# A hyena filter prepared in thirteen buffers of its own and copied out whole: gated recurrence and long convolution on one core

## The chip, the core and the metric

The kernel runs on one core of one Trainium2 chip. The metric is device time in microseconds (us) from the start of a launch to its end; less is better. The engines of a core that matter here are PE (TensorE, the matmuls; PEld is its loading of weights), DVE (VectorE), ACT (ScalarE), POOL (GpSimd) and SP (SyncE, which here only issues DMA transfers). PSUM is the memory that PE writes, in 8 banks of 512 float32 per partition; SBUF is the working memory of 128 partitions; HBM (also called DRAM below) lies outside the core.

## The reference

Two models in a chain. The first is a gated recurrence over 6272 time steps, the second multiplies two projections of its result with a third one that was convolved with a filter of full length.

```python
# x, f_logit: (4, 6272, 256); lower_bound: (256)
sig = 1.0 / (1.0 + np.exp(-f_logit))
f = lower_bound + (1.0 - lower_bound) * sig
for t in range(S):
    h = f[:, t] * h + (1.0 - f[:, t]) * x[:, t]
    y[:, t] = h
# second model, x = y: w_proj (256, 768), filter_fft (6272, 256), w_out (256, 256)
proj = x @ w_proj
x1, x2, x3 = proj[..., :D], proj[..., D:2*D], proj[..., 2*D:]
X2 = np.fft.rfft(x2, n=S, axis=1)
H = np.fft.rfft(filter_fft, n=S, axis=0)
x2_conv = np.fft.irfft(X2 * H, n=S, axis=1)
out = (x1 * x2_conv * x3) @ w_out
```

All inputs and the output are float32.

## The kernel before

*The transform.* S = 6272 = 128 x 49 (`M` and `Q`), so a transform of the whole length is done as two rounds of matmuls, over 128 and over 49, with tables of sines. What has no partner in this split, frequency 0 of each row, is carried by a small extra path ("mini", "zm", "slot").

*Preparation (`prepare`), once.* The filter comes from HBM in 13 groups of four values of r (0 to 48; `ff`, L619), each 128 x 1024 float32, 0.524 MB. They go into 10 buffers in turn (`raws`, L438 to L442, and L618: `raws[g % len(raws)]`): seven in the space of `X2`, two in `Hu`, one in `HA`; groups 10, 11 and 12 wait until a buffer is free. A cast writes a group to one of two halves of `afs` (`fr`, L625), a matmul per r rotates it (`rot`, L630, with the table `rot` that `turns` copies from the identity), and two copies per group (`f2`, L634), one per half p of the columns, take it from PSUM to one of two tiles `f2`. The first transform of the filter (`FF1`, L655, 16 steps u of 8 columns pairs, two ops each) needs all 13 groups of its half of the columns; a copy (`afs`, L660), the second transform (`FF2`, L673) and a copy (`hw`, L677) follow; every two steps the spectrum is stored to a table in DRAM (`hst`, L682) of 192 rows: 128, and once more 64 in turned order. Later each batch loads a step's spectrum back with `turned` (L276), 128 rows from row 0 and 128 from row 49. The zero frequency is done by `last` (L691).

The tables are computed on the chip: integers (`iotas`, POOL, L487 on), arguments folded into one period (`args0`, `args1` and `fold`, DVE, L515 on), a sine on ACT, then the tables `D1r` and `FTr` for the filter ("tabs": three DVE and two POOL operations) and `D1`, `FT`, `VA`, `VB`, `ID` for the batches ("rest", POOL). Their scratch space lies in `A` and `PP`. The weights are scaled by 1 - lower_bound and cast to half precision by seven ACT operations ("W", L477 to L487). PE runs 24 fillers (`warm`, L600, four matmuls on the identity, nothing reads them); before, 10 of them stand ahead of the first FF1 and 14 at the very end.

*Recurrence (`hgrn`, L319), per batch.* 13 chunks of 512 steps: loads of f_logit and x (L332) into slots, a sigmoid (ACT, L335), u = sigmoid * x (POOL, L337), transposes for two halves kh of the channels (`su`, PE, L349), f (`f`, ACT L362 or DVE L364), the scan (DVE, L370) into `HA`. The first 3072 steps of `HA` are copied once more behind its end ("wrap", L379, on ACT, POOL or by a DMA of SP), as the circular convolution reads past it. Batch 0 has four slots for its input: three of its own and one in `XS`, the space where x1 and x3 are laid later; batches 1 to 3 have three.

*Convolution, per batch.* `phase_p` projects x2 (P, L714, 13 groups of four r, each needs all scans) and copies it to `X2` ("x2"). 16 units u follow: F1 (L727) with the copy A, F2 (L790), the product with the spectrum, which is loaded by SP into `Hu` (three places and one more in `Hl`, "H", L768), then the back transform I2 (L832) and the copy `Th`. The product is either made by DVE straight from PSUM (L813, in the order table MUL) or by a copy on ACT or DVE and a multiply on POOL (`pm`, L822). `gate` makes x1 and x3 (x13, PE, L398): x1 is copied to `XS`, and x3 is either multiplied straight from PSUM by DVE (L419) or copied, with the product z on POOL (L428). `phase_o` does the last transform (I1, L895), the product with z (y, DVE, L901), the output projection (proj, L913), a copy ("o") and the store (L925). The scans of the next batch run under the units and the gate of this one.

*What sets the order.* No scheduler works at build time. Every piece of work is an operation `op(kind, cost, ...)` with a number; the table `ORDER` (a string of base 64 digits at the top of the file) lists for all 2429 operations their number, engine and PSUM bank, and `Plan.emit` issues them in that order. `cost` names the engines on which an operation may run; which one it gets stands in the table. Each engine and SP's queue of transfers work strictly in the order of the table. The core of it:

```python
for i, e, b in self.order():
    o = self.ops[i]
    assert e in o["cost"] and i not in seen and o["preds"] <= seen
    ...
    o["fn"](*args)
```

Of the kernel before, what the change touches and what calls it, by code (L numbers as in the profile page):

```python
# [2 lines left out]

# [6 lines left out]
F32 = mybir.dt.float32  # L10
F32R = mybir.dt.float32r
F16 = mybir.dt.float16
# [48 lines left out]
class Plan:  # L61
# [63 lines left out]
    "AAYAvQAeQAOYAzYAiQAnQAoQA0gA1AAfQA5gA6YA+gAqQBDgAjQBIgBNgABIACIAPIARIAQAAUIAWIA2QA/YA3AA4AATIA7SBEYBXgA8CA9CBAUB"  # L125
    "JYBCEBFWBOYBHGBBEBGGBKQBLABMIBPSBYYBQCAVYAXYBSgBTAAwUBRKAdUBZUBaEBUWBWGBVOBhgBiYBcgBdYBjQBbEBeSBgCBkABrgBsIBtUAS"
    "ABmgBnIBoWBfKBuEBwgBxIBySBvEBpOBqOBzCB5UB6MAYYAZYADgEGgB0CD6gD8AD7gB3SB+WB4KD5gAEYB/OB1YBlICAUCBECJSEIAEHgB8WB9G"
    "B7YCKKCCYD9YEegCDQCEIEJYESgETgCQUEgACHSCREAFgCOWCIKCLYCPOCSYD+QEUACMSCNCCTUCUEEfgAGgECWEqgErgCZSCaCCGgD/IEAIEDOE"
    "EOEVYEKQCXUEhYAHACeSELAAIAEOWE3gE2gCYMCbYCfCEMIEPGEQOAJACgUCcSChECiYCdCEWQCjUCkEEaWFCgAaYCpSEXIEYIEbGEcOCqCEsACW"
    "gEiUEjMEtYCmgCnQCoAFDgCrYCwSEkMCuWCxCCvGCyYEmQEnIFMgFNgCzSE4AEoIE5YC0CCsUCtEEuWGJgEZYEvOFEAFFYCFgEySFWgEzKFXgC3Q"  # L130
    "C4AEwOExYC5UC6EE0KALAE6QC7YE7AFOADAUC+WDBMFPYC/GDCYE8IE9YE+SFggE/CFhgFAKC8UC9EAKAFGWFHGDDQDEIDFgFIODHUDIEAMAE1YF"
    "BYFJSFKCFqgDJQFrgEdYEpgDKIDLYDOUFYAFZYDPEDQWDRGB2YFQQFTUF0gF1gFLKFiADSYDMSDNCDTWDUGFaSFRIC1gFUMFSIFbCDXQDgWDYAFV"
    "MFcKFjYDZUFdQANADaMDbYDhOFsAF/gFtYFkSFeAFfIDcUFlCFmKDdEF+gDVgFnWMsgMtgF2AClgDeQDfIDnUFoGDoEFpOFuSFvCDjQFwKDkAFxU"
    "M5gFyEFzMDpWDqGM4gF3YF4QF5AF6IF7SDiYDrYGAAJdWGIgJfGDuUEBYDwWF8CGBYDvEEFYDxGDyYERYF9KJeQJiRJgoGCUGFWElYJhYJkBMggM"
    "hgGGGGHOGDEGEMC2gENADsSDGgDzQD0ID3WDtCD1gD2gD4OGZUGaECVgGbSMuAGcCGfQGgAGhUGiMMiAMjYM6AGLWGdSGeKGMGGNQGOAGVUGWMM7"
    "YGPSGQKJjWJluJmYJnXGjQGkAMvYGXUDmgGYEGTQGKgGUAJpPGRSGSKDWgJoUJsVJtQJxRJqEJrYJzJJvADlgGrSGlWJyUGmOJuFJwYJ2VGsCGnQ"
# [58 lines left out]
def kernel(  # L195
# [801 lines left out]
```

## Time and profile before

| | us |
|---|---|
| runs of the kernel before | 459.30, 458.43, 457.25 (median 458.43) |
| span of the profiled execution | 455.6 |
| first rotation of the filter starts | 6.28 |
| first FF1 starts | 22.82 |
| last input of batch 0 has landed | 64.75 |
| last scan of batch 0 starts | 70.8 |
| first P of batches 0, 1, 2, 3 | 71.5, 167.1, 266.0, 366.0 |
| last output projection ends | 450.4 |
| last store lands | 454.2 |

The page shows one profiled execution; its span runs from the first to the last instruction, and the runs without a profile are some 2 to 4 us longer than that. The groups of the page's fifth part give the count, the busy time and the mean of one operation by line and form; the ones with most time on each engine are these:

```profile
L337 POOL TENSOR_TENSOR XT<-XT,FL 128x1024 f32<-128x1024 f32 (+1 forms) x49 | 109.9, 2247 | 55.7 <-ACT FL L335 38.5
L370 DVE TENSOR_TENSOR_SCAN HA<-fTs,HA,PS 128x512 f16<-128x512 f32 (+1 forms) x96 | 112.7, 1202 | 2.0 <-ACT fTs L362 1.1
L398 PE MATMUL PS<-HA,W 128*128 128x490 f16 (+1 forms) x416 | 100.2, 367 | 0.3 <-ACT Th L284 0.2
...
L284 ACT CAST HA<-PS 128x1024 f16<-128x1024 f32 (+1 forms) x101 | 81.2, 831 | 3.3 <-POOL PP L822 0.8
```

So the 96 scans take DVE 112.7 us, 1.202 us each, and before them DVE stood idle for 2.0 us in all, mostly until ACT had written `fTs`. Nearly all the copies from PSUM go through one helper, `copy`, whose lines are L284 and L286 on ACT and the like on DVE; there the tile, not the line, tells what is copied.

### The profile page before, as it was taken

The page shows a single profiled execution, that of the slowest core. Times are in us where ns is not written, and L with a number is a line of the kernel's source. Part 1 is how long each engine was busy: PE and PEld are TensorE (multiplying, and loading weights), DVE is VectorE, ACT ScalarE, POOL GpSimd, SP SyncE. Part 2 cuts the span into 40 slices and gives each one's busy share as a digit, 9 for nine tenths or more (in the row PEclk, how much of TensorE's full clock was granted, in tenths as well). Part 3 has the DMA queues.
Part 4 walks back from the last instruction along what each step waited for, and adds up shares of the span by engine and source line. Part 5 has one row for each costly group of instructions (what it writes and reads, how often), then busy time and mean ns, then how long its engine had stood idle before and what let it go on. Part 6 is the DMA issues. An engine that isn't in the chain of part 4 may idle for free.

```text
span 455.6 us, 14635 instructions
## 1 busy us (share of the span) xinstructions
PE 439.6 (96%) x6009; PEld 348.4 (76%) x6009; DVE 407.4 (89%) x476; ACT 402.3 (88%) x577; POOL 308.8 (68%) x279
## 2 busy tenths in 40 slices
PE   7899999999999999999999999999999999999998
PEld 5687778677767888777668888777778896776797
DVE  8899997799999996999999977999999976989873
ACT  5899999899999987899989998999989858987563
POOL 8888973878899542788995626899994405696400
PEclk9599999999999999999999999999999999999999
DMA  8999999767898985479776896778759721765186
GB/s 326 387 371 345 378 375 361 279 187 233 299 300 282 340 300 237 169 232 374 253 264 219 285 315 272 237 250 303 261 177 317 301 95 46 248 187 185 47 321 246
DMA packets 44434, 120.74 MB, mean 265 GB/s; under 512 B 4304, under 2 KB 7632, under 8 KB 44368
## 3 DMA queue, kind: packets, MB, share of 16 engines
q1 hardware_dynamic: 44368, 119.82, 74.5%
q8 instruction: 47, 0.77, 0.7%
q14 instruction: 19, 0.16, 0.1%
HBM read 86.12 MB, written 31.98 MB: 259 GB/s over the span
## 4 chain that ended last, share of the span: by engine, by line
PE 72%; DVE 11%; ACT 9%; issue 4%; DMA 3%; POOL 1%; SPq 0%; ACTq 0%; DVEq 0%; POOLq 0%
PE PS L398 17%; PE PS L714 9%; PE PS L832 9%; PE PS L913 8%; PE PS L790 7%; DVE HA L370 7%; PE PS L727 6%; PE PS L349 6%; PE PS L895 4%; ACT fTs L362 2%; DMA X<-in_moe_filter_fft_dram 2%; PE PS L600 2%; ACT HA L284 2%; DVE ys L901 1%; ACT X L284 1%
## 5 line engine op out<-in xcount | busy, mean ns | idle before, releaser
L337 POOL TENSOR_TENSOR XT<-XT,FL 128x1024 f32<-128x1024 f32 (+1 forms) x49 | 109.9, 2247 | 55.7 <-ACT FL L335 38.5
L370 DVE TENSOR_TENSOR_SCAN HA<-fTs,HA,PS 128x512 f16<-128x512 f32 (+1 forms) x96 | 112.7, 1202 | 2.0 <-ACT fTs L362 1.1
L398 PE MATMUL PS<-HA,W 128*128 128x490 f16 (+1 forms) x416 | 100.2, 367 | 0.3 <-ACT Th L284 0.2
L822 POOL TENSOR_TENSOR PP<-HA,Hu 98x1008 f16<-98x1008 f16 x42 | 88.0, 2106 | 5.6 <-ACT HA L284 2.6
L284 ACT CAST HA<-PS 128x1024 f16<-128x1024 f32 (+1 forms) x101 | 81.2, 831 | 3.3 <-POOL PP L822 0.8
L901 DVE TENSOR_TENSOR ys<-PS,zt 128x1024 fp32r<-128x1024 f32 (+1 forms) x52 | 58.3, 1151 | 14.0 <-PE PS L895 10.3
L813 DVE TENSOR_TENSOR PP<-PS,Hu 98x1008 f16<-98x1008 f32 x54 | 63.6, 1199 | 1.5 <-PE PS L790 0.7
L362 ACT ACTIVATE fTs<-PS,nomc 128x512 f32<-128x512 f32 (+1 forms) x90 | 59.5, 680 | 4.5 <-PE PS L349 4.2
L398 PEld LDWEIGHTS <-W 128*128 128x128 f16 x416 | 35.3, 97 | 30.2 <-issue 2.9
L428 POOL TENSOR_TENSOR zt<-XS 128x490 f16<-128x490 f32 (+1 forms) x26 | 31.8, 1223 | 39.0 <-DVE ys L901 27.4
L913 PE MATMUL PS<-Wo,ys 128*128 128x256 f32 x392 | 57.5, 293 | 0.4 <-DVE ys L901 0.3
L286 ACT ACTIVATE XS<-PS 128x490 f32<-128x490 f32 (+1 forms) x88 | 51.0, 590 | 6.8 <-DVE zt L419 2.6
L832 PEld LDWEIGHTS <-PP 98*128 98x128 f16 x1024 | 49.2, 98 | 10.1 <-POOL PP L795 1.3
L284 ACT CAST Th<-PS 128x784 f16<-128x784 f32 x63 | 52.0, 828 | 3.4 <-PE PS L832 2.7
L913 PEld LDWEIGHTS PS<-Wo,ys 128*128 128x128 f32 x392 | 49.6, 188 | 4.5 <-DVE ys L901 1.2
L832 PE MATMUL PS<-VA,PP 98*128 98x98 f16 x512 | 52.1, 207 | 0.2 <-POOL PP L795 0.2
L832 PE MATMUL PS<-VB,PP 98*128 98x98 f16 x512 | 51.8, 207 | 0.0
L419 DVE TENSOR_TENSOR zt<-PS,XS 128x490 f16<-128x490 f32 (+1 forms) x78 | 49.2, 648 | 2.7 <-ACT XS L286 0.8
L335 ACT ACTIVATE FL<-FL 128x1024 f32<-128x1024 f32 (+1 forms) x49 | 49.8, 1022 | 0.6 <-DMA FL<-in_f_logit_dram 0.6
L714 PE MATMUL PS<-W,HA 128*128 128x256 f16 x392 | 44.6, 273 | 1.1 <-ACT X L284 1.1
L714 PEld LDWEIGHTS <-HA 128*128 128x128 f16 x392 | 42.9, 142 | 2.0 <-issue 1.3
L349 PE MATMUL PS<-iden,FL 64*128 64x64 f32 x736 | 41.7, 229 | 2.6 <-ACT PP L286 0.6
(119 smaller groups left out, 778.7 us busy)
## 6 DMA issues: line engine op xcount, KB each, us to landing
FL<-in_f_logit_dram SPq DMA_DIRECT2D x45, 512.0 KB, 5.3
XT<-in_x_dram SPq DMA_DIRECT2D x45, 512.0 KB, 6.2
Hu<-H SPq DMA_DIRECT2D x39, 512.0 KB, 4.6
out_dram<-osb SPq DMA_DIRECT2D x24, 512.0 KB, 4.6
out_dram<-PP SPq DMA_DIRECT2D x16, 512.0 KB, 4.8
Hl<-H SPq DMA_DIRECT2D x13, 512.0 KB, 4.7
X<-in_moe_filter_fft_dram SPq DMA_DIRECT2D x9, 512.0 KB, 7.0
out_dram<-HA SPq DMA_DIRECT2D x8, 512.0 KB, 5.7
```

What stands on the lines that cost most here:

```text
L284: nc.scalar.copy(dst, src)
L337: op("u", {"POOL": 0.1 + 0.553 * nb}, lambda e, xt=xt, ft=ft: nc.gpsimd.tensor_tensor(xt, xt, ft, op=AOP.mult), r=[("ft", k)], w=[("xt", k)])
L349: nc.tensor.transpose(bank(pb)[:, at[p] + j:at[p] + hn:nb], src[ps, j, cols], iden[ps, ps])
L362: nc.scalar.activation(fT, sT, AF.Identity, scale=by, bias=1.0)
L370: nc.vector.tensor_tensor_scan(h, fT, bank(pb)[:, 512 - hn:512 + hn], init, op0=AOP.mult, op1=AOP.add),
L398: nc.tensor.matmul(PS[:, p, 0:n], W13[:, kh, js], HA[:, HB[kh] + t0:HB[kh] + t0 + n], start=(kh == 0), stop=(kh == 1))
L714: nc.tensor.matmul(pp[:, r - r0, :], column(HB[kh], q_of(r)), W2[:, kh, :], start=(kh == 0), stop=(kh == 1))
L813: nc.vector.tensor_tensor(pr, px.unsqueeze(1).broadcast_to([TB, 2, UE, 63]), hh(), op=AOP.mult)
L822: nc.gpsimd.tensor_tensor(pr, spec[:, o, :, 1:64].unsqueeze(1).broadcast_to([TB, 2, UE, 63]), hh(), op=AOP.mult)
L832: nc.tensor.matmul(PS[:, ib + o, pr * TB:(pr + 1) * TB], PP[:TB, k, o, n, 2 * pr:2 * pr + 2, :], v[:TB], start=(n == 0), stop=(n == 1))
L901: nc.vector.tensor_tensor(late["ys"][:, yk, :, 0:rn * 128], PS[:, cb:cb + 2, 0:rn * 128], late["zt"][:].rearrange("p k r m -> p k (r m)") ...
L913: nc.tensor.matmul(po[:, i, :], late["ys"][:, yk, kh, i * 128:(i + 1) * 128], Wo[:, kh, :], start=(kh == 0), stop=(kh == 1))
```

## The change

*Filter.* 13 buffers instead of 10 (`raws`): seven in `X2`, three in `Hu`, one in `HA`, two in `A`; every group has its own. One tile `f2` for all columns; a group is copied out by one operation (`runs`) instead of two, and each FF1 needs all 13 whole groups.

*Tables.* Their scratch moves from `A` and `PP` to the part of `HA` that the recurrence reaches with chunk 6 and later (`st`). `D1r` is made by ACT and `FTr` by POOL in the new table; `turns` stands behind `args0` on DVE, the memset of `FT` moves from the integers on POOL to an operation of its own on DVE, and the weights' casts "W" may run on POOL or DVE as well and run on POOL in the new table.

*Spectrum.* The table in DRAM has 160 rows instead of 192 (the second store has 32 rows), and a load brings 98 rows to 98 partitions instead of 128 to 128. `Hl`, `Th` move from the scope that closes with the last FF2 to the one that closes with the last FF1, both output buffers `osb` the other way.

*Input of batch 0.* Three slots in the space of `X2` instead of one in `XS`, six in all (`slots0`), with loads in the order 0 to 5, 0 to 4, 0, 1; `XS` is free from the start. The zeroing of `X2`'s gaps, `last` and its copy into `X2` move behind the recurrence of batch 0 (`finish`).

*Small things.* "zm" is one operation instead of two; "wrap" may run on DVE too (it never does in the new table); a sigmoid waits for the tables' sine.

*Order.* A new `ORDER`, 2418 operations. All 24 fillers stand ahead of the first FF1. By kind, changes in the engine: x3 straight from PSUM on DVE 77 times before, 90 after; copies x1 and x3 on ACT 111, after 99; x2 on DVE 20, after 25; Th on DVE 1, after 6; A on DVE 10, after 6; wraps of all batches on ACT 8, after 0, of batch 0 on POOL 10 and SP 1, after 5 and 7. The diff, cut to its core, without the table:

```diff
-    H = [dram.tile([2, M + 64, 2 * UE * 64], F16, name=f"H{u}") for u in range(NU // 2)]
+    H = [dram.tile([2, M + 32, 2 * UE * 64], F16, name=f"H{u}") for u in range(NU // 2)]
     def turned(a):
         return bass.AP(tensor=a.tensor, offset=a.offset,
-                       ap=[[a.ap[0][0], M], [Q * a.ap[0][0], 2], a.ap[1]])
+                       ap=[[a.ap[0][0], TB], [Q * a.ap[0][0], 2], a.ap[1]])
...
-    more = [[v.rearrange("p (j d) -> p j d", d=D) for v in vs] for vs in (
-        [XS[:, i * 1024:(i + 1) * 1024] for i in range(2)],)]
-    more_t = (["xsf"] + [("x1s", j, i) for j in range(2) for i in range(2)],)
+    more = [[X2[:, i * 2048:(i + 1) * 2048].bitcast(F32).rearrange("p (j d) -> p j d", d=D)
+             for i in range(2 * j, 2 * j + 2)] for j in range(3)]
+    more_t = [[("raw", 2 * j), ("raw", 2 * j + 1)] for j in range(3)]
+    slots0 = (0, 1, 2, 3, 4, 5, 0, 1, 2, 3, 4, 0, 1)
...
-                k = c % (NX + len(more))
+                k = slots0[c]
...
-                ft, ft, AF.Sigmoid, scale=-1.0), w=[("ft", k)], table="sigmoid")
+                ft, ft, AF.Sigmoid, scale=-1.0), r=["sin"], w=[("ft", k)], table="sigmoid")
...
-                   r=["xsf"] + (["cz", ("x1s", j, 0)] if direct else []),
+                   r=["cz", ("x1s", j, 0)] if direct else [],
...
+                 for i in range(NK)]
+        raws += [(HA[:, S + 1024:S + 3072], [("W", 0, 1), ("W", 0, 2)])]
+        raws += [(HA[:, A0 + i * 2048:A0 + (i + 1) * 2048], [t for j in (2 * i, 2 * i + 1) for t in At(j) + Ax(j)])
                  for i in range(2)]
-        raws += [(HA[:, S + 1024:S + 3072], [("W", 0, 1), ("W", 0, 2)])]
...
-            op("W", {"ACT": 0.6}, lambda e, kh=kh, by=by: act.activation(
+            op("W", {"ACT": 0.6, "POOL": 0.7, "DVE": 0.6}, lambda e, kh=kh, by=by: copy(
...
-        scr, st = HA[:, A0:A0 + AW], [("At", i) for i in range(NA)]
-        ti = scr[:, 0:2004].bitcast(I32)
-        w = scr[:, 2016:4080].bitcast(F32)
-        v = PP[:].rearrange("p k e a i n -> p (k e a i n)")[:, 0:2064].bitcast(F32)
+        st = [("hn", kh, c) for kh in range(2) for c in range(6, NCHK)]
+        ti = HA[:, HB[0] + WR:HB[0] + WR + 2004].bitcast(I32)
+        w = HA[:, HB[1] + WR:HB[1] + WR + 2064].bitcast(F32)
...
-            raw, et = raws[g % len(raws)]
+            raw, et = raws[g]
...
+        def runs(r0, rn):
+            a = f2[:, r0:r0 + rn]
+            return bass.AP(tensor=a.tensor, offset=a.offset,
+                           ap=[a.ap[0], [NEP // 2 * PF, 2], [PF, NEP // 2], [64, 2], a.ap[1]])
...
-            for p in range(2):
-                op("f2", either(128 * rn), lambda e, pb, r0=r0, rn=rn, p=p: copy(
-                    e, both(fv[p][:, :, r0:r0 + rn]),
-                    PS[:, pb:pb + 2].rearrange("m a (r e) -> m (a r) e", e=256)
-                    [:, 0:rn, p * 128:(p + 1) * 128].rearrange("m r (e g) -> m g e r", e=2)),
-                   r=["f2e"], w=[("f2", g, p)], src=rt)
+            op("f2", either(256 * rn), lambda e, pb, r0=r0, rn=rn: copy(
+                e, runs(r0, rn), PS[:, pb:pb + 2].rearrange("m a (r e) -> m (a r) e", e=256)
+                [:, 0:rn].rearrange("m r (p e g) -> m p g e r", p=2, e=2)),
+               r=["f2e"], w=[("f2", g)], src=rt)
...
-                        r=[("f2", g, u // 8) for g in range(13)] + ["D1r", "f2e"],
+                        r=[("f2", g) for g in range(13)] + ["D1r", "f2e"],
...
-            for i, (p0, n, to) in enumerate(((0, M, 0), (M - TB, 64, M)) if u % 2 else ()):
+            for i, (p0, n, to) in enumerate(((0, M, 0), (M - TB, 32, M)) if u % 2 else ()):
...
-            for e2 in range(2):
-                nc.vector.tensor_tensor(
-                    zp[:TB, q % 2, e2],
-                    PS[:TB, pb + e2, 0:2 * n].rearrange("p (k i) -> p k i", k=2)
-                    .unsqueeze(1).broadcast_to([TB, 2, 2, n]),
-                    Hm[:TB, e2, :, :, es], op=AOP.mult)
+            nc.vector.tensor_tensor(
+                zp[:TB, q % 2],
+                PS[:TB, pb:pb + 2, 0:2 * n].rearrange("p e (k i) -> p e k i", k=2)
+                .unsqueeze(2).broadcast_to([TB, 2, 2, 2, n]),
+                Hm[:TB, :, :, :, es], op=AOP.mult)
...
-        op("pre", {"SP": 0.01}, turn_head, r=FF1[:NU], w=["cz"])
-        op("pre", {"SP": 0.01}, turn, r=FF1 + FF2 + ["ID", "VA", "FT1", "D1", "VB", "cz"], w=["cv"])
+        op("pre", {"SP": 0.01}, turn_head, r=FF1, w=["cz"])
+        op("pre", {"SP": 0.01}, turn, r=FF2 + ["cz", "ID", "VA", "FT1", "D1", "VB"], w=["cv"])
```

More of the change, by code (lines that the diff above doesn't have):

```diff
@@ L597, in warm @@
+        op("rest", {"POOL": 1.6, "DVE": 0.6}, rest1, r=["v0", "FT0", "cols1"] + st, w=["FT1", "VA"])
+        op("rest", {"POOL": 1.0, "DVE": 0.7}, rest2, r=["v1", "cols1"] + st, w=["ID"])
         def warm(e, p, i):
@@ L905, in phase_o @@
                    op=AOP.mult),
-               r=[("z", jb, c) for jb in range(2) for c in range(NCHK)],
+               r=["cv"] + [("z", jb, c) for jb in range(2) for c in range(NCHK)],
                w=[("y", yk)], src=i1)
```

307 lines of the change are left out of this document (151 added, 156 removed).

## The prediction

> **What bounds the kernel now.** I read the page first (busy shares, the chain), then the table of windows cut where the work changes (the first FF1 at 22.8 us, the first projection P at 71.5, then the P of each batch), then the timeline of the first 24 us, then the groups by line and form. The durations below are means of those groups.
>
> ```profile
> PE 439.6 (96%) x6009; PEld 348.4 (76%) x6009; DVE 407.4 (89%) x476; ACT 402.3 (88%) x577; POOL 308.8 (68%) x279
> PE 72%; DVE 11%; ACT 9%; issue 4%; DMA 3%; POOL 1%; SPq 0%; ACTq 0%; DVEq 0%; POOLq 0%
> ```
>
> No engine has much room, and the chain runs through PE for 72% of the span. The windows (PE, PEld, DVE, ACT, POOL busy, clock, DMA share, GB/s) tell the stages apart:
>
> ```profile
> 0.00:22.80 22.80, 18.21 (x89) 14.19 (x89) 18.93 (x49) 15.56 (x25) 19.55 (x40) 0.78 0.93 357
> 22.80:71.50 48.70, 45.93 (x598) 36.52 (x599) 47.19 (x53) 48.49 (x75) 40.84 (x44) 1.00 1.00 368
> 71.50:167.10 95.60, 93.80 (x1375) 72.76 (x1373) 88.50 (x97) 91.09 (x132) 70.86 (x54) 1.00 0.84 281
> 167.10:266.00 98.90, 96.47 (x1421) 77.13 (x1419) 92.57 (x101) 90.24 (x131) 68.46 (x53) 1.00 0.74 260
> 266.00:366.00 100.00, 98.46 (x1453) 78.72 (x1450) 91.81 (x103) 93.33 (x132) 73.00 (x55) 1.00 0.76 268
> 366.00:455.60 89.60, 86.72 (x1086) 69.05 (x1082) 68.39 (x79) 63.60 (x87) 36.06 (x34) 1.00 0.49 171
> ```
>
> Up to 22.8 us a chain sets the pace: filter group from DMA, cast, rotation on PE, copy, and FF1 only when all groups are there. From 22.8 to 71.5 ACT (48.49 of 48.70 us) and DVE (47.19) set it, with DMA full beside them. After that PE does (375.5 of 384.1 us). The early part in the timeline:
>
> ```profile
> 4.68 1.27 DVE L517 TENSOR_SCALAR PP<-HA 128x520 f32<-128x520 f32 x1
> 5.99 1.28 DVE L518 TENSOR_SCALAR PP<-PP 128x520 f32<-128x520 f32 x1
> 7.31 1.44 DVE L519 TENSOR_TENSOR PP<-HA,PP 128x520 f32<-128x520 f32 x1
> ...
> 12.44 0.42 DVE L517 TENSOR_SCALAR PP<-HA 128x512 f32<-128x512 f32 x1
> 12.89 0.43 DVE L518 TENSOR_SCALAR PP<-PP 128x512 f32<-128x512 f32 x1
> 13.35 0.69 DVE L519 TENSOR_TENSOR PP<-HA,PP 128x512 f32<-128x512 f32 x1
> ```
>
> The same three operations take 3.99 us while POOL runs casts and 1.54 us when POOL waits. On PE:
>
> ```profile
> 6.28 1.50 PE L630 MATMUL PS<-afs,rot 128*128 128x256 f32 x8
> ...
> 13.26 1.89 PE L600 MATMUL PS<-iden 128*128 128x256 f16 x8
> 15.00 2.07 PE L630 MATMUL PS<-afs,rot 128*128 128x256 f32 x8
> 17.44 4.61 PE L630 MATMUL PS<-afs,rot 128*128 128x256 f32 x17 [0.37 <-POOL afs L296]
> 22.82 1.45 PE L655 MATMUL PS<-D1r,f 128*128 128x256 f32 x10 [0.77 <-ACT f L284]
> ```
>
> **Part 1, up to the first FF1.** *Own buffers for 13 groups:* the transfers already run back to back (0.524 MB lands every 1.27 us from 4.46 to 18.55 us, the small last one at 18.93), so earlier issue lands nothing earlier: 0, covered by the full DMA (0.93 share). *Whole groups:* before, 24 copies of 512 elements at 0.685 us and two of 128 at 0.468, 17.4 us; after, 7 on ACT of 1024 at 1.04, 5 on DVE at 1.22 and one at 0.41, 13.8 us. 3.6 us less over two engines; but FF1 now waits for the whole groups. *Tables:* three DVE operations (1.62 us) leave for ACT and POOL. *`turns`* (0.35 us) moves behind the first `args`, so the first rotation cannot start at 6.28; it starts at 8.75 + 0.35 = 9.1 us if that block stays slow, or at 6.65 if its three folds run at 1.54 us (POOL then has no cast to do, since `fr` waits for the rotations). DVE's queue behind `args`: five copies at 1.22, one at 0.41, four `fr` at 0.73, 9.4 us; from 14.04 this ends at 23.4, from 11.6 (14.04 − 2.45) at 21.0. *Fillers:* 24 instead of 10 lie ahead of FF1, 14 × 0.437 = 6.1 us more of PE, in time that PE had idle or spent at half clock. I take FF1 at 22.3, −0.5, between −1.8 and +1.5 (POOL is nearer to idle during the first folds, its casts nearer to busy during the second).
>
> **The clock.** In before the granted clock is 1.00 up to about 11.3 us and 0.50 until about 21.5, though PE's longest idle stretch there is 0.71 us; over the 3.4 us before the fall PE did three groups of rotations of 0.54 us weight-load time, about half of the time. Fillers cost 0.437 us at full clock and 0.945 at half. The extra fillers may keep the clock up, which would shorten each rotation from 1.08 to some 0.6 us; this is in the −1.8. The Trainium skill ("TensorE: Matmul & The Clock Gate", HAM oscillation) says that the clock falls after an idle stretch of some 3.4 us; here the trace differs, since it fell with no idle stretch over 0.71 us. By that rule the changed kernel would keep its clock and the part would be worth up to −1.8; by the row it can fall again.
>
> **Part 2, from FF1 to P (48.7 us).** DVE: afs 12 to 9 (−3 × 0.676), hw 4 to 1 (−3 × 1.21), f 9 to 13 (+4 × 0.737), xs +1 (0.66): −2.0 us. ACT: seven weight casts W leave (2 × 0.776 + 4 × 0.474 + 0.622 = 4.07), f 17 to 13 (−4 × 0.706), one wrap (−0.61); afs +3 (0.604), hw +2 (1.04), xs +2 (0.59), one sigmoid of the next batch (1.06): −1.4. Both were full, so the smaller counts: −1.4. POOL takes the seven W: its rows of tensor_scalar (98 elements 0.572, 256 elements 0.928) give by a straight line 1.5 for 512 and 0.64 for 128, so 2 × 1.5 + 4 × 0.64 + 0.55 = 6.1 us, and gives five wraps back (3.1): +3.0, covered by its 7.9 us of idle time. Behind a W on POOL stand `u`, then su on PE, f and the scan; without that cover one W of 1.5 us is late once, so the part lies between −2.0 and +1.5.
>
> DMA in this stage: spectrum stores shrink by 32 rows × 2 × 2 KB × 8 = 1.05 MB (−2.5 us at 0.524 MB per 1.27 us), six wraps more go to SP (6 × 131 KB, +1.9 us): −0.6, hidden behind ACT and DVE. On SP each wrap waits for its scan, and the loads behind it wait too: 48 transfers stand ahead of the last load in both orders, and six input slots instead of four let loads start earlier; 0. Spectrum loads shrink from 128 to 98 rows, 52 times; hidden, since products wait for PE and ACT (wait table), not for H. The Trainium skill ("DMA: Bandwidth & Descriptors", on the semaphore's 16) says a transfer uses the largest number of engines up to 16 that divides its rows: 98 rows use 14, so by the rule a load falls by 12.5% per engine and not by 23%; no run here shows 98 rows yet, and at 0 by either the sum stays.
>
> **Part 3, after P (384.1 us).** PE's work is the same; the 14 fillers at the end lay in waits and are worth 0 (the last store came from ACT). Counts from the order table. DVE: products xs 77 to 90 (+13 × 0.658), x2 20 to 25 (+5 × 1.22), Th +5 (0.965), prod copies +2 (0.68), o +1 (1.2); A −4 (1.22), xs copies −4 (0.65), f −1 (0.74); zm one operation instead of two (0.74 to about 0.47, on the line from 128 elements at 0.372 to 490 at 0.658; 16 × −0.27): +9.6. ACT: wraps −8 (0.613), xs −12 (0.59), x2 −5 (1.05), Th −5 (0.828), prod −2 (0.605), sig −1, o −1; A +4 (1.03), f +1, hw +1: −18.8. POOL: z 26 to 14 (−12 × 1.23), wraps +2, one pad: −12.9. Of their 341.3, 338.3 and 248.4 us this is +2.8%, −5.6% and −5.2%. What lies on the path I take from the chain's shares (DVE 50 us, ACT 41, POOL 4.6): +1.4 − 2.3 − 0.2 = −1.1. Bounds: no more can be won than PE's 8.6 us without work; no more lost than DVE's whole 9.6.
>
> **Sum.** −0.5 − 1.4 − 1.1 = −3.0 us on a span of 455.6, 452.6. Around that span lie 458.4 − 455.6 = 2.8 us to the median of the runs, so 455.4.
>
> **Rivals.** (1) *DVE becomes the bound, slower.* The extra products stand in the stretch where x13 and the scans of the next batch meet, and there DVE has nothing left (100 to 160 us: 19.66, 19.43 and 19.87 of 20). Then all 9.6 count against parts 1 and 2 (−1.9): 458.4 + 7.7 = 466. For it: DVE's 89%, and scans that feed everything. Against it: 42.8 us of idle DVE after P. It decides once DVE idles under 1% in each batch's second half. (2) *The clock falls among the fillers.* If it falls at 11.3 us as before, some 9 rotations at 1.085 and 6 fillers at 0.945 remain: FF1 at 11.3 + 9.8 + 5.7 = 26.8, +4.0 instead of −0.5: 459.9, no measurable change or just slower. For it: the same clock row; against it: fillers fill the gaps that let it fall. (3) *The table only shuffles.* PE has 8.6 us without work after P, spread over all batches, and the start moves by nothing: 458. (4) *Part 1 or 2 does not do as said:* FF1 at +1.5, POOL's W late, +1.5, and the rest as forecast: 460.3.
>
> **Chances.** Forecast 0.42 (455.4, its own range 449 to 457.5); (1) 0.22; (2) 0.12; (3) 0.16; (4) 0.08. Half a per cent, 2.3 us, is about what a measurement can tell from no change. Faster 0.42; slower: (1), most of (4) and a third of (2), 0.32; same 0.26. The range, 449 to 466, goes up to (1) and down to part 3 at −7.5 us.
>
> **What would show it.** Right: first FF1 at 22 to 23 us with granted clock 1.00 through the first 22 us; P at 69 to 70.5 us; from P to P at 94 to 99 us, DVE some 350 us busy after P and ACT 320; POOL's waits shorter. Wrong: clock 0.50 beside L600 rows of 0.9 us per four and FF1 past 24; PE waiting for DVE's scans or L419/L420 products in the wait table; loads of H landing late.

## The result and the profile after

The changed kernel takes 475.4 us (median; 474.1 to 477.3) beside 457.9 us for the kernel before on the same chip: ratio 1.038, interval 1.034 to 1.042. It is slower, by more than the range allowed. The profiled execution's span is 475.5 us, against 455.6; it is the longest of the four executions of after, so the spans differ by 19.9 us and the medians by 17.5. The busy line and the chain of waits of its page:

```profile
PE 440.3 (93%) x6009; PEld 345.8 (73%) x6009; DVE 418.1 (88%) x473; ACT 390.6 (82%) x535; POOL 297.5 (63%) x268
...
PE 52%; DMA 15%; DVE 13%; ACT 9%; issue 6%; POOL 3%; SPq 1%; DVEq 0%; ACTq 0%; POOLq 0%
```

PE has the same work, but its part of the chain falls from 72% to 52%; DMA's grows from 3% to 15%, DVE's only from 11% to 13%. The table of windows, cut at the same events (first FF1, first P of each batch; PE, PEld, DVE, ACT, POOL busy, clock, DMA share, GB/s):

```profile
0.00:27.30 27.30, 19.44 (x145) 16.12 (x145) 20.07 (x47) 15.77 (x16) 18.68 (x36) 1.00 0.95 369
27.30:80.20 52.90, 48.55 (x598) 37.17 (x599) 45.75 (x51) 47.88 (x68) 44.11 (x46) 0.97 0.80 285
80.20:180.60 100.40, 93.97 (x1372) 73.07 (x1373) 91.22 (x96) 86.44 (x121) 64.63 (x52) 0.98 0.77 252
180.60:282.90 102.30, 96.75 (x1419) 76.40 (x1417) 92.87 (x99) 89.90 (x126) 70.07 (x55) 1.00 0.72 238
282.90:386.50 103.60, 99.98 (x1441) 78.50 (x1440) 96.61 (x104) 89.20 (x124) 67.40 (x48) 0.98 0.72 251
386.50:475.50 89.00, 81.62 (x1041) 64.50 (x1038) 71.58 (x79) 61.39 (x83) 32.64 (x32) 0.98 0.44 159
```

Of the 19.9 us, 4.5 come before the first FF1 (27.3 against 22.8), 4.2 from there to the first P (52.9 against 48.7), 4.8, 3.4 and 3.6 in the three batches that follow, and −0.6 in the last one, which loads no input for a batch behind it.

*Up to FF1.* The timeline of the copies of rotated groups, with the idle time of the engine and its releaser in brackets:

```profile
15.57 2.34 ACT L280 CAST f<-PS 128x1024 fp32r<-128x1024 f32 x2 [1.48 <-DVE f L285]
...
17.95 2.55 DVE L285 CAST f<-PS 128x1024 fp32r<-128x1024 f32 x2 [1.21 <-ACT f L280]
...
20.61 3.57 ACT L280 CAST f<-PS 128x1024 fp32r<-128x1024 f32 x3 [2.19 <-DVE f L285]
...
24.21 1.23 DVE L285 CAST f<-PS 128x1024 fp32r<-128x1024 f32 x1 [2.24 <-ACT f L280]
25.52 1.13 ACT L280 CAST f<-PS 128x1024 fp32r<-128x1024 f32 x1 [1.35 <-DVE f L285]
26.69 0.60 DVE L285 CAST f<-PS 128x256 fp32r<-128x256 f32 x1 [1.25 <-ACT f L280]
27.34 2.05 PE L646 MATMUL PS<-D1r,f 128*128 128x256 f32 x12 [2.99 <-DVE f L285]
```

All thirteen copies run one after the other from 11.70 to 27.29 us. At every change of engine the next copy waits for the one on the *other* engine, though they write different columns; the last rotation had ended at 24.3, so PE idles for 2.99 us.

*SP's queue.* SP's part of the timeline shows the second loss:

```profile
51.10 0.42 SPq L673 DMA_DIRECT2D H<-Hu  x1
51.56 0.43 SPq L331 DMA_DIRECT2D X<-in_f_logit_dram  x1
58.47 0.52 SPq L290 DMA_DIRECT2D HA<-HA  x1
59.09 0.53 SPq L331 DMA_DIRECT2D X<-in_x_dram  x1
59.67 0.44 SPq L673 DMA_DIRECT2D H<-Hu  x1
60.16 0.47 SPq L290 DMA_DIRECT2D HA<-HA  x1
60.74 1.17 SPq L331 DMA_DIRECT2D FL<-in_f_logit_dram  x1
62.01 1.14 SPq L331 DMA_DIRECT2D XT<-in_x_dram  x2
```

SP issues nothing from 52 to 58.47 us: at its head stands a wrap (`HA<-HA`) into space that a weight cast on POOL still reads until 58.4, and loads stand behind it. DMA is not idle meanwhile: its engines are busy for 0.72 of the stop, with transfers issued before. A stop from 26.6 to 40.0 us, behind a load whose slot was not free, lies before it; there DMA does run dry, with 11 GB/s from 35 to 40 us. After the first P, loads stand likewise behind stores, wraps and spectrum loads that are not ready. For each input load issued after the first P I took the time from the end of the last operation that frees its slot to its issue: on average 0.68 us in before and 2.08 us in after. The wait table of after has rows that before has at 0.6 us (sigmoid) or not at all (products). First the row of before, then those of after:

```profile
ACT FL L335 <- DMA FL<-in_f_logit_dram: 0.6, 1, 0.6
```

```profile
ACT FL L334 <- DMA FL<-in_f_logit_dram: 9.3, 7, 2.6
...
POOL PP L823 <- DMA Hl<-H: 2.4, 1, 2.4
DVE PP L814 <- DMA Hl<-H: 2.3, 2, 1.4
DVE PP L814 <- DMA Hu<-H: 2.0, 1, 2.0
POOL PP L823 <- DMA Hu<-H: 1.9, 3, 0.9
```

(us in total, times, longest.) POOL's wait for x is no longer than it was (9.3 us, 11.8 in before). The busy times of DVE and POOL changed much as priced, ACT's fell by less, so the question is which of these waits is the cause.

### The profile page after: what moved, and what is told of

Same layout as the page of the kernel before. It is cut to its first block, busy times and chain, and to the rows that moved or that the text cites. A ratio compares the mean times of both kernels' runs of the same rounds, so it can differ in the third digit from the quotient of the medians.

```text
span 475.5 us, 14551 instructions
## 1 busy us (share of the span) xinstructions
PE 440.3 (93%) x6009; PEld 345.8 (73%) x6009; DVE 418.1 (88%) x473; ACT 390.6 (82%) x535; POOL 297.5 (63%) x268
## 4 chain that ended last, share of the span: by engine, by line
PE 52%; DMA 15%; DVE 13%; ACT 9%; issue 6%; POOL 3%; SPq 1%; DVEq 0%; ACTq 0%; POOLq 0%
PE PS L398 12%; DMA FL<-in_f_logit_dram 7%; PE PS L348 7%; PE PS L833 6%; PE PS L914 6%; PE PS L716 5%; PE PS L791 4%; DMA Hu<-H 4%; DVE HA L369 4%; PE PS L729 3%; PE PS L896 3%; DVE PP L814 3%; PE PS L646 3%; DMA out_dram<-osb 2%; POOL XT L336 2%
## 5 line engine op out<-in xcount | busy, mean ns | idle before, releaser
L336 POOL TENSOR_TENSOR XT<-XT,FL 128x1024 f32<-128x1024 f32 (+1 forms) x47 | 104.9, 2236 | 67.3 <-ACT FL L334 46.3
L398 PE MATMUL PS<-HA,W 128*128 128x490 f16 (+1 forms) x416 | 103.4, 371 | 2.7 <-ACT HA L282 1.0
L823 POOL TENSOR_TENSOR PP<-HA,Hu 98x1008 f16<-98x1008 f16 x43 | 90.1, 2104 | 10.9 <-ACT HA L280 2.8
L280 ACT CAST HA<-PS 128x1024 f16<-128x1024 f32 (+1 forms) x103 | 83.0, 831 | 11.1 <-PE PS L729 6.9
L361 ACT ACTIVATE fTs<-PS,nomc 128x512 f32<-128x512 f32 (+1 forms) x87 | 56.9, 669 | 5.3 <-PE PS L348 3.4
L419 DVE TENSOR_TENSOR zt<-PS,XS 128x490 f16<-128x490 f32 (+1 forms) x90 | 57.3, 653 | 2.4 <-PE PS L398 0.8
L334 ACT ACTIVATE FL<-FL 128x1024 f32<-128x1024 f32 (+1 forms) x47 | 47.3, 1011 | 9.4 <-DMA FL<-in_f_logit_dram 9.3
L280 ACT CAST Th<-PS 128x784 f16<-128x784 f32 x58 | 47.2, 817 | 5.3 <-PE PS L833 4.4
L348 PE MATMUL PS<-iden,FL 64*128 64x64 f32 x704 | 40.6, 231 | 4.3 <-ACT osb L282 1.9
L348 PEld LDWEIGHTS PS<-iden,FL 64*128 64x128 f32 x704 | 30.9, 140 | 16.0 <-ACT osb L282 2.7
```

Source lines behind the costliest of these rows:

```text
L280: nc.scalar.copy(dst, src)
L336: op("u", {"POOL": 0.1 + 0.553 * nb}, lambda e, xt=xt, ft=ft: nc.gpsimd.tensor_tensor(xt, xt, ft, op=AOP.mult), r=[("ft", k)], w=[("xt", k)])
L348: nc.tensor.transpose(bank(pb)[:, at[p] + j:at[p] + hn:nb], src[ps, j, cols], iden[ps, ps])
L398: nc.tensor.matmul(PS[:, p, 0:n], W13[:, kh, js], HA[:, HB[kh] + t0:HB[kh] + t0 + n], start=(kh == 0), stop=(kh == 1))
L419: nc.vector.tensor_tensor(zd(), px, xs(0), op=AOP.mult)
L823: nc.gpsimd.tensor_tensor(pr, spec[:, o, :, 1:64].unsqueeze(1).broadcast_to([TB, 2, UE, 63]), hh(), op=AOP.mult)
```

## The experiments

All ratios are to the kernel before on the same chip, with 95% intervals; one per cent is 4.6 us. "P to P" gives the distances from the first P of batch 0 to that of 1, 2, 3 and to the end of the span: 95.6, 98.9, 100.0, 89.5 in before, 100.4, 102.3, 103.6, 89.0 in after.

**The filter's copies, and three wraps.** `e1_merged` writes the same bytes of `f2` in the same order with a target of three free dimensions instead of four:

```diff
-                           ap=[a.ap[0], [NEP // 2 * PF, 2], [PF, NEP // 2], [64, 2], a.ap[1]])
+                           ap=[a.ap[0], [PF, NEP], [64, 2], a.ap[1]])
```

> The changed kernel, with the target of the whole-group copies written with three free dimensions ([PF, 128], [64, 2], [1, rn]) instead of four; the bytes, the table and the engines are the same. Theory A (the 13 copies into f stand in one line, each waiting for the one before on the other engine, because the four-dimensional target is not told apart from the others): the copies overlap on ACT and DVE, first FF1 at 22.5 to 24 us instead of 27.3, PE's clock no longer falls at 27 us, first P 3 to 6 us earlier (74 to 77), time 468 to 471. Theory B (the copies alternate because each waits for its own rotation and PE's banks): FF1 stays at 27 and the time at 475.

Measured: 471.9 us, 1.030 (1.026 to 1.033), 0.85 of a per cent below after. First FF1 at 24.3 us, first P at 75.7, P to P 98.1, 101.8, 104.7, 89.3. The copies in its timeline now overlap, and wait for PE's rotations:

```profile
14.85 1.23 DVE L285 CAST f<-PS 128x1024 fp32r<-128x1024 f32 x1 [2.73 <-PE PS L631]
15.08 2.20 ACT L280 CAST f<-PS 128x1024 fp32r<-128x1024 f32 x2
17.34 2.34 DVE L285 CAST f<-PS 128x1024 fp32r<-128x1024 f32 x2
...
24.31 1.65 PE L646 MATMUL PS<-D1r,f 128*128 128x256 f32 x12 [0.86 <-DVE f L285]
```

So the pattern of the target made copies on two engines wait for each other. That its overlap with the other groups is not seen in four dimensions is the reading that fits; shown is only that the waits go with the pattern.

`e2_wraps_late` (on after) and `e3_both` (on e1) move the three wraps that hold SP up before 72 us:

```diff
 order table, by position: number, kind, engine
-274: 292 wrap SP   284: 288 wrap SP   288: 240 wrap SP
+the same three directly ahead of position 330: 268 wrap SP
```

> The changed kernel with three entries of the order table moved: the wraps of batch 0 that SP issues at 58.5, 60.2 and 63.3 us stand behind the last input load of batch 0. Theory A (SP's queue stands from 52 to 58.5 us at a wrap that waits for the weight cast on POOL, and holds the last five loads): last load of batch 0 lands 4 to 6 us earlier (66 to 68 instead of 72.1), first P 2 to 4 us earlier, time 471 to 473.5. Theory B (those loads have time, and ACT, DVE and POOL set the stage): first P within 1 us of 80.2, time 474 to 476.

> Both edits. Theory A (what comes after the first P is late because the start is late: the loads of batch 1 and the spectrum stores pile up in the DMA queue): first FF1 at 23, first P at 71 to 73, and from the first P to the end 384 to 388 us instead of 395, time 458 to 462. Theory C (after the first P the extra products on DVE cost their 10 us whatever the start does): first P at 71 to 74, but 393 to 396 us from there to the end, time 467 to 470.

Measured: e2 477.9 us, 1.042 (1.037 to 1.047); e3 472.7, 1.030 (1.023 to 1.037). The first P comes earlier (77.7 for 80.2; 73.6 for 75.7), but P to P is 101.0, 102.2, 107.7 in e2 and 99.1, 100.8, 103.2 in e3, and no time is won. (e3's profile is of its shortest execution, 467.6 us; the others took 472.3 to 474.6, so its P to P are on the low side.) Loads of batch 0 were late, but what holds up the later batches is something else.

**Is DVE the bound?** `e4_both_x3` (on e3) takes 13 of the x3 products from DVE to a copy on ACT and a multiply on POOL:

```diff
 order table
-607, 612, 617, 632, 652, 657, 682, 1170, 1185, 1200, 1693, 1708, 1713: xs, product straight from PSUM on DVE
+the same numbers: xs, copy on ACT, with their z on POOL behind them
```

> Both edits, and 13 of the 90 x3 products that DVE makes straight from PSUM go back to a copy on ACT and a product on POOL (7 in batch 0, 3 each in batches 1 and 2), placed where they stood; DVE loses 8.5 us, ACT gains 6.6, POOL 16. Theory C (DVE is what bounds after P): 4 to 8 us less than the kernel with both edits. Theory A: within 2 us of it, or slower.

Measured: 494.2 us, 1.080 (1.075 to 1.086). DVE's busy time falls to 412.0 us (418.1 in after); the wait table has a new row:

```profile
POOL zt L490 <- ACT XS L342: 34.6, 11, 9.5
```

POOL stands in its queue before those z for 34.6 us, with u of the next batch behind them. This does not clear DVE; it shows that engines cannot be exchanged in place. `e6_dve_less` and `e7_act_less` (on e1) therefore take work away and move nothing: 13 products of z on DVE, or the 13 copies of x1 beside them on ACT, handle one element in ten or in eight (parts of z, or of x1, are left out), which takes 3.7 us from DVE (13 times 0.659 − 0.371) and 4.2 from ACT (13 times 0.588 − 0.263):

```diff
+                    if less:
+                        nc.vector.tensor_tensor(zd()[:, :, 0:1], px[:, :, 0:1], xs(0)[:, :, 0:1], op=AOP.mult)
-                    if e == "MUL":
+                    elif e == "MUL":
...
+                    k = 1 if less else n // Q
-                    copy(e, xs(0), PS[:, p, 0:n].rearrange("p (m r) -> p r m", r=Q), ZS)
+                    copy(e, xs(0)[:, :, 0:k], PS[:, p, 0:n].rearrange("p (m r) -> p r m", r=Q)[:, :, 0:k], ZS)
```

> The changed kernel with the three-dimensional target, in which 13 of the x3 products on DVE (7 in batch 1, 6 in batch 2) are made for one tenth of their columns only, so that much of z is left out and the output is not the reference's: DVE has 7 us less in these two batches. Theory C (DVE bounds the stretch from P to P): batches 1 and 2 together 5 to 7 us shorter than in the kernel with the three-dimensional target alone (101.7 + 104.7 us there). Theory D (late loads in the DMA queue set it): less than 2 us shorter.

> The same, but in the same 13 places the copy of x1 on ACT is made for one tenth of its columns and the product is whole; x1 is left out there in part, so that the output is not the reference's: ACT has 6 us less in batches 1 and 2. Theory C (DVE bounds): less than 2 us shorter. Theory E (the queue of ACT, from which f, x2 and A wait, bounds): 4 to 6 us shorter.

Measured: e6 473.2 us, 1.033 (1.029 to 1.037); e7 472.3 (465.9 to 474.1, too far apart for an interval); e1 had 1.030. P to P 99.3, 104.5, 105.5 and 99.1, 101.9, 104.9. Less work on DVE or on ACT wins nothing. The amounts are close to what these intervals can show (0.8 and 0.9 per cent); what settles it for DVE is e14 below. The clock is no cause either: in e1 it stands at 1.00 in each of the first three batches, which are still 304.6 us long in all, against 294.5 in before.

**The spectrum alone.** `b1_spectrum` is the kernel before with 160 rows, loads of 98 rows and "zm" as one operation:

```diff
-    H = [dram.tile([2, M + 64, 2 * UE * 64], F16, name=f"H{u}") for u in range(NU // 2)]
+    H = [dram.tile([2, M + 32, 2 * UE * 64], F16, name=f"H{u}") for u in range(NU // 2)]
-                       ap=[[a.ap[0][0], M], [Q * a.ap[0][0], 2], a.ap[1]])
+                       ap=[[a.ap[0][0], TB], [Q * a.ap[0][0], 2], a.ap[1]])
...
```

> The kernel before with one part of the change alone: spectrum of 160 rows, loads of 98 rows, zm as one operation; its table is untouched. Theory O: 457 to 459 us, as before (smaller loads are hidden, zm saves 1 us of DVE). Theory K: 4 to 9 us slower, since the loads of 98 rows or the joined zm hold up the products.

Measured: 458.7 us, 1.001 (0.998 to 1.003). The part is worth nothing, as forecast, and takes nothing.

**The order.** `e5_old_order` and `e9_old_from_p1` (on e1) take engines and order of the kernel before, e5 from batch 0's first P on, e9 from batch 1's. At the joint of e5 one copy reads a bank that the next product has written over, so part of that output differs; the work is the same.

```diff
 order table
-everything behind the first P of batch 0 (e5) or batch 1 (e9): after's engines and order
+the same operations: engines and order of before
```

> The changed kernel with the three-dimensional target of the filter copies, and with two tables joined: up to the first P the new one, from there on order, engines and PSUM banks of the old one. Theory O (the 8 to 10 us after the first P come from the new table: more products on DVE, loads that stand behind other loads and spectrum loads in SP's queue): from the first P to the end 384 to 387 us, time 461 to 464. Theory K (they come from the code: loads of 98 rows, the joined zm, other buffers): 392 to 395 us, time 469 to 472.

> The changed kernel with the three-dimensional target, the new table up to the first P of batch 1 and the old one (order, engines, PSUM banks) from there. Theory O (the new table itself costs the time after P, in many small waits, since it fits the lengths of the operations less well): P1 to P2 98.5 to 100.5 us instead of 101.8, P2 to P3 99 to 101 instead of 104.7, time 463 to 466. Theory K (the changed code costs it): 101 to 102, 104 to 105, time 471 to 473.

`e8_fewer_fillers` (on e1) moves 6 of the 14 fillers ahead of the first rotation to the end:

```diff
 order table
-1 to 41: 17 fillers, 14 of them ahead of the first rotation
+1 to 41: 11 fillers, 8 of them ahead; six behind the last operation
```

> The changed kernel with the three-dimensional target, and six of the 14 fillers that stand on PE ahead of the first rotation put at the end of the table. Theory F (the fillers hold the first rotation back: they end at 9.2 us, its cast at 5.4 and its table rot at 7.2): first rotation at 7.2 to 7.6 us instead of 8.9 to 9.9, first FF1 1 to 2 us earlier (22.2 to 23), time 469.5 to 471. Theory G (copies and casts set the pace of the filter groups, and the clock needs the fillers): first FF1 unchanged or later, with granted clock under 1.00 before 22 us.

Measured: e5 469.0 us, 1.022 (1.018 to 1.026), P to P 100.0, 101.7, 99.2, 89.1; e9 464.6, 1.015 (1.011 to 1.019), 98.9, 100.8, 99.4, 89.2. With the old table batch 2 comes down to the time of before (99.2 and 99.4 for 104.7 in e1); batches 0 and 1 do not (100.0 and 101.7 in e5), and from the first P to the end e5 takes 389.9 us, between what theories O and K gave. So the new table lengthens batch 2; that it does so to the others too, and that the code does not, e14 shows below. e8: 476.6, 1.039 (1.035 to 1.044): the first rotation is 2.5 us earlier (7.32 for 9.86), FF1 only 0.6, P to P 96.2, 100.5, 108.1, 91.4. Of this 2.1 us more lie behind the last P, where the fillers now stand behind the last output copy; batch 2 is longer too, in a profile whose clock fell there (0.86 from 325 to 350 us), so the total is no clean test of the fillers.

`e10_sp_sorted` and `e11_small_loads` ask which part of the table. e10 (on e1) changes SP's sequence alone, from 72 us on: loads and spectrum loads stand where e1's profile says that their place becomes free. e11 (e1's table) lets the input loads of batches 1 to 3 bring a quarter of their bytes (three quarters of that input are left out):

```diff
 SP's part of the table around batch 0's first P (lo1: load of batch 1, hs: spectrum store, pr: set-up)
-lo1 hs hs hs pr lo1 hs pr lo1 H H lo1 hs hs hs
+lo1 hs hs hs pr lo1 lo1 hs pr lo1 H lo1 lo1 H hs
```

```diff
+                k0 = 1 if b in (1, 2, 3) else nb
...
-                    dst, src[b, t0:t0 + n, :].rearrange("(p j) d -> p j d", p=128)),
+                    dst[:, 0:k0], src[b, t0:t0 + n, :].rearrange("(p j) d -> p j d", p=128)[:, 0:k0]),
```

> The changed kernel with the three-dimensional target and SP's part of the table sorted anew from 72 us on: loads of inputs and of the spectrum stand in the order in which their places come free in the trace, so that none waits behind another that isn't free yet; all other engines as they are. Theory D (late loads set the stages): a load waits 0.7 us on the mean instead of 2.0 after its place is free, P to P 2 to 4 us shorter in each of batches 0 to 2, time 462 to 467. Theory O: within 2 us of 472.

> The changed kernel with the three-dimensional target, where the loads of x and f_logit of batches 1 to 3 bring one row of four only (the rest of the slot keeps old values, so that the output is not the reference's): 0.13 MB each instead of 0.52, landing about 3 us sooner. Theory D (loads): from the first P to the end 385 to 389 us instead of 393.8, time 463 to 467. Theory O: within 2 us of 472.

Measured: e10 465.5 us, 1.016 (1.013 to 1.019), P to P 99.6, 99.8, 100.0, 89.1; e11 459.9, 1.006 (1.002 to 1.010), P to P 94.9, 99.4, 99.9, 89.0. With engines and all other queues as in after, sorting SP's queue wins as much as the whole old table in e9, and input that arrives sooner wins still more. In e10 a load after the first P is issued 0.24 us after its place is free (e1: 2.04).

`e12_sp_all` sorts SP from 25 us on, spectrum loads among each other too. `b2_sp_sorted` sorts the *old* table from 72 us on. `e13_w_on_act` is e12 with the weight casts on ACT. `e14_sp_again` is e12, but the spectrum loads stand in the order that they have in e10:

```diff
 SP's part of the table, e12 against e14
-hs H wrap pr H lo1 lo1 pr lo1
+hs wrap pr lo1 lo1 pr H lo1 lo1
 e13 against e12
-7, 10, 8, 9, 11, 12, 13: W POOL
+7, 10, 8, 9, 11, 12, 13: W ACT
```

> The changed kernel with the three-dimensional target and SP's part of the table sorted by readiness from 25 us on: inputs of batch 0 no longer stand behind a load whose place isn't free or behind wraps that wait for weight casts, spectrum stores go out some 8 us after they are ready. Theory D (the loads' lateness sets stage after stage, the one up to the first P and batch 0 too): last input of batch 0 lands before 64 us, first P at 72 to 74, P0 to P1 96 to 98, time 457 to 462. Theory H (ACT, DVE and POOL set the stretch from FF1 to P, the loads have time there): first P at 75 to 76, time 463 to 466 as with the sort from 72 us on.

> The kernel before, with SP's part of its table sorted in the same way from 72 us on. Its loads stand 0.7 us behind their places on the mean, in the new table 2.0. Theory D, carried over: 0 to 2 us faster than before (456 to 458). If the old table is as good as its engines allow: 457.5 to 459.

> The same with the seven weight casts back on ACT, at their places in the order. Theory W (casts on POOL, 6 us of it, hold u and the transposes back, and wraps and loads with them): first P 1 to 3 us earlier, time 1 to 3 us less than without. Theory V (POOL had room, ACT hasn't): first P 1 to 4 us later.

> The sort from 25 us on once more, but with the spectrum loads left in their order among themselves; in the kernel before this one a spectrum load whose place came free at 98.9 us stood ahead of two whose places were free at 92.3 and 96.2, and SP stood still from 84 to 99 us. Theory D (what stands late in SP's queue sets batch 0): first P at 74 to 75 us, P0 to P1 96 to 98, time 459 to 463. Theory H (batch 0 is set by something else): P0 to P1 99 to 100, time 463 to 466.

Measured: e12 478.1 us, 1.044 (1.040 to 1.047); b2 457.6, 0.9996 (0.998 to 1.001); e13 481.9, 1.052 (1.047 to 1.056); e14 461.2, 1.008 (1.004 to 1.012). In e12 batch 0 takes 107.3 us, and the next two batches 101.3 and 104.1. SP's timeline and the wait table in that batch show one block:

```profile
83.92 16.22 SPq L767 DMA_DIRECT2D Hu<-H  x4
```

```profile
POOL PP L821 <- DMA Hu<-H: 4.2, 1, 4.2
```

SP spends 16 us on four spectrum loads: a load that was not wanted yet (number 484, into a place still being read) stands ahead of two that were. e14 has it behind them:

```profile
75.10:170.90 95.80, 92.27 (x1373) 72.63 (x1373) 90.56 (x96) 85.80 (x121) 64.34 (x52) 1.00 0.75 247
170.90:269.80 98.90, 96.52 (x1419) 76.32 (x1417) 92.77 (x99) 89.54 (x126) 69.92 (x55) 1.00 0.70 236
269.80:369.60 99.80, 98.23 (x1441) 77.00 (x1439) 96.28 (x104) 88.99 (x124) 67.35 (x48) 1.00 0.79 266
369.60:458.80 89.20, 81.67 (x1043) 64.52 (x1038) 71.74 (x79) 61.69 (x83) 32.65 (x32) 0.97 0.44 159
```

```profile
PE 69%; DVE 9%; DMA 7%; ACT 7%; issue 5%; POOL 2%; SPq 0%; DVEq 0%; ACTq 0%; POOLq 0%
```

```profile
ACT FL L332 <- DMA FL<-in_f_logit_dram: 1.7, 2, 1.2
```

(windows, chain and waits of e14). The stages after P are those of before again, with after's engines and after's code: DVE does as much work as in after, so it is not the bound, and neither is the code; ACT's wait for f_logit falls from 9.3 to 1.7 us, PE's share of the chain is 69%. b2 shows that such a sort is not a gain by itself: in the old table it brings the loads from 0.68 to 0.17 us behind their places and wins nothing. e13 brings the first P 3.8 us later than e12 (78.4 for 74.6): ACT has less room for the casts than POOL.

**What is left.** e14's first FF1 is at 24.6 and its first P at 75.1 us, before's at 22.8 and 71.5. `e15_start` (on e14) and `e16_w_dve` (on e15):

```diff
 order table, e15
-14 fillers, then the first rotation; turns behind args0 on DVE
+8 fillers, then the first rotation; six behind the last operation; turns ahead of args0
 e16
-W POOL
+W DVE
```

> The kernel with SP's loads put in order from 25 us on, and 6 of the 14 filler entries ahead of the first rotation moved to the end of the stage, with two argument operations of ScalarE behind the rotation copies. If the start of the chain of rotations and copies sets the first FF product, the first rotation goes from about 8.9 to 6.5-7.3 us, the first FF product from 24.6 to 23-23.8, and the time comes 1 to 1.5 us down, to about 459.5-460. If the casts and copies set the pace, the first FF product stays at 24-24.6 and the time within 0.5 us of the run before (461). P to P stays at 95.8, 98.9, 99.9 by both.

> As the run beside it, with the weight casts W on VectorE as in the kernel before, rather than on POOL. If the 1.8 us that the stretch from the first FF product to the first P of batch 0 is still longer comes from the casts standing in POOL's queue ahead of u and z, the first P comes 1 to 2 us sooner and the time falls by as much. If VectorE is as full there as POOL, nothing changes or the first P comes up to 2 us later.

Measured: e15 464.3 us, 1.013 (1.010 to 1.017); e16 467.2, 1.020 (1.016 to 1.025). In e15 the first FF1 is at 22.9 and the first P at 73.3: fillers and `turns` had set the start. (ACT's part of the table is as in e14; the operations that stand behind `turns` now are DVE's.) But the end does not follow: batch 0 takes 98.4 instead of 95.8, and the last lines of SP and PE read

```profile
452.61 1.40 SPq L924 DMA_DIRECT2D out_dram<-HA  x1
...
457.06 4.38 PE L596 MATMUL PS<-iden 128*128 128x256 f16 x24 [3.59 <-ACT osb L280]
```

The six fillers at the end wait for the last output copy and lengthen the span by about 2.7 us (91.8 against 89.1). The 2.6 us of batch 0 come late in it: until 133 us its work takes as long as in e14. Then ACT waits twice for a load of f_logit, where e14 has one wait of 0.58 us. In e15:

```profile
140.77 1.85 SPq L329 DMA_DIRECT2D FL<-in_f_logit_dram  x1
...
146.71 1.06 ACT L332 ACTIVATE FL<-FL 128x1024 f32<-128x1024 f32 x1 [2.03 <-DMA FL<-in_f_logit_dram]
...
159.29 1.06 ACT L332 ACTIVATE FL<-FL 128x1024 f32<-128x1024 f32 x1 [1.72 <-DMA FL<-in_f_logit_dram]
```

In e14:

```profile
142.54 0.38 SPq L329 DMA_DIRECT2D FL<-in_f_logit_dram  x1
...
147.03 1.06 ACT L332 ACTIVATE FL<-FL 128x1024 f32<-128x1024 f32 x1 [0.58 <-DMA FL<-in_f_logit_dram]
```

SP issues the first of these loads as soon after the first P as in e14, but the issue takes 1.85 us instead of 0.38, in the one profile of each; why is not shown. e16's first P is at 77.1, 3.8 us later than e15's: DVE is a worse place for the casts than POOL. (In before they stand on ACT, not on VectorE as the expectation has it.) Whether the casts on POOL cost something between FF1 and P stays open.

No version run here beats the kernel before.

## Why the prediction was wrong

It gave 455.4 us, from −0.5, −1.4 and −1.1 us; by the spans it was +4.5, +4.2 and +11.2.

*Part 1 (to FF1): wrong at "whole groups".* The durations were nearly right (1.13 to 1.19 us on ACT where 1.04 was taken, 1.23 on DVE), but "3.6 us less over two engines" holds only if two engines work at once, and they did not: 3.0 of the 4.5 us (27.3 to 24.3 in e1). The rest is in "fillers": I put all of the extra ones into time in which PE was idle; 14 rather than 8 stand ahead of the first rotation and start it at 8.93 instead of 6.28 us, inside the span I gave for `turns`, but it costs 0.6 us by itself (e8 against e1) and 1.7 with `turns` ahead of DVE's argument operations (24.6 to 22.9 in e15). The clock stayed at 1.00 through 25 us, and a rotation took 0.59 to 0.74 us, near the forecast (0.6).

*Part 2 (FF1 to P): wrong at SP's queue, put at 0.* "48 transfers stand ahead of the last load in both orders" counts what stands ahead, not when it may go. SP stopped twice, for 13 and 6.5 us, with loads behind the head of its queue. Of the 4.2 us, e1 removes 1.5: in after the clock is 0.71 and 0.82 from 27.3 to 35 us, behind PE's idle time at FF1, and in e1 it is 1.00 there, so this part goes with the copies (that the clock is the reason is argued, not tested). SP's queue is worth 0.9 (e14 against e1) to 2.4 us (e2 against after), by single profiles; 1.8 stay open. W on POOL cost 6.4 us (estimated 6.1), and ACT and DVE are worse places for it (e13, e16).

*Part 3 (after P): DVE and POOL were priced nearly right, the queue that feeds the engines not at all.* DVE rose by 11.0 us after P (341.3 to 352.3; forecast 9.6), POOL fell by 13.6 (12.9), ACT only by 11.3 (forecast 18.8). Operations on ACT overlap in the records (in before those after P add up to 381 us in 338 us of busy time), so counts times mean times give too much there. With SP's sequence mended (e14) the stages sum to 383.7 us, 0.4 below before: about the −1.1 forecast. The failing step is that the part's cost was taken from counts of operations and the chain's shares alone; the order of the loads after P was never looked at. SP's sequence is worth 2.2 per cent, some 10 us (1.030 to 1.008).

*The rivals.* (1), DVE as the bound, had the sign and came nearest (466), for a reason that e14 refutes: it has the same products on DVE, and the stages of before. (2) did not happen: at the start the clock fell only after PE's idle time at FF1. It fell again later in after (at 93 and 380 us, for 3.4 us each, and behind the last product), but not in e1's first three batches, which are nearly as long. (3) underrated the table. (4) had the place of part 1 and a third of its size. What was missing is a rival for which the profile of before had a row: DMA, at 3% of the chain, hidden by an order in which a load stood 0.68 us behind its free slot on the mean. The chance of 0.32 for slower was too small, as the order was replaced whole and only the engines' share of it was examined.

*What stays open.* 1.8 us between FF1 and P (by single profiles; b1, with before's table, has 50.6 us there too, against 48.7 in before); and why, with the start restored in e15, f_logit comes late in batch 0, which takes 2.6 us longer, so that the gain is gone by batch 1's first P.

## What to carry to other kernels

In a kernel whose queues follow a written order, compare the order of each queue as well as the counts: for each transfer, when its place is free against when it is issued, and what stands ahead of it; a transfer that is not ready blocks all behind it, whatever DMA has to spare. When copies on two engines write one tile, look at the releasers in brackets: a wait for the other copy rather than for the producer means that they run in turn, and a target pattern of fewer dimensions can undo it, as in e1. Work put in "idle" time has a price if it stands ahead of the first link of a chain, or behind the last.

## What the runs showed of the hardware

*The clock.* Windows of after:

```profile
15.00:20.00 5.00, 2.52 (x20) 2.21 (x19) 3.69 (x5) 2.82 (x3) 3.70 (x5) 1.00 1.04 406
...
25.00:27.30 2.30, 0.00 (x0) 0.00 (x0) 1.03 (x2) 1.76 (x2) 0.70 (x1) 1.00 0.98 401
27.30:30.00 2.70, 2.50 (x14) 2.21 (x15) 1.26 (x2) 2.69 (x4) 0.89 (x1) 0.71 1.03 421
30.00:35.00 5.00, 5.00 (x43) 3.79 (x43) 2.61 (x4) 3.64 (x6) 3.17 (x7) 0.82 0.87 349
```

With PE busy for half of the time from 15 to 20 us the clock stays at 1.00; it falls just after 2.99 us of idleness. In before it is lower with PE busy for 4.13 of 5 us:

```profile
10.00:15.00 5.00, 4.13 (x20) 2.80 (x20) 4.76 (x14) 5.00 (x10) 3.37 (x4) 0.63 1.03 410
```

So the busy share of a few microseconds does not tell by itself when it falls. The Trainium skill ("TensorE: Matmul & The Clock Gate", HAM oscillation) puts the fall behind an idle stretch of about 3.4 us: after is near that; before, with no idle stretch over 0.71 us until then, is not.

*98 rows.* A spectrum load of 98 rows leaves 15 updates of its completion count instead of 16, and the table of transfers of the profile's page gives no landing times for after. The first update comes 0.5 us after the issue, the other 14 from about 3 us after it. The Trainium skill ("DMA: Bandwidth & Descriptors", on the semaphore's 16) has 14 engines for 98 rows, one update each, and one by the issuer for the rest: 15, so the trace agrees. From issue to landing a load takes 5.01 us in b1 and 5.01 us with 128 rows in before, each the mean of 52 loads: 23% fewer bytes made them no sooner on the mean.
